# Attention and a gated feed-forward layer on one core: the output product in fifteen block products instead of seven

## The chip, the cores and the metric

The kernel runs on one core of a Trainium2 chip. The metric is the device time of one execution in microseconds (us), lower is better. TensorE (PE) does the matmuls into eight PSUM banks of 512 fp32 columns, VectorE (DVE) and ScalarE (ACT) the elementwise work, GpSimd (POOL) a part of it in the attention, and SyncE (SP) issues all transfers on one queue.

## What is computed

```python
scores = scale * q @ k.T + bias          # 8 x 8 heads, 576 tokens, head size 64
attn = softmax(where(mask, scores, -1e9))  # causal, window of 128
x = (attn @ v) -> [4608 tokens, 512]
gate = 1.0 / (1.0 + np.exp(-(x @ w_gate)))   # 512 x 1536
val = x @ w_val
out = (gate * val @ w_out)                   # 1536 x 512
```

All results are fp32. The weights come in fp64 and are decoded on the chip to fp32.

## The kernel before

The program is recorded as a graph of operations (`Graph.add`). `Graph.order` then chooses, with a cost written for each operation, which operation each engine issues next: the one that can start first, and among near equals the one with the smaller due time `want`. `SHIFTS` is a table of numbers that moves the due times of groups of operations. The instruction order on each engine is fixed by this when the program is built; on the chip each engine runs its own list and waits on semaphores.

There are three stages. In the **early stage** (to about 284 us) the attention of 32 pairs of heads runs beside the first third of the gate and value products (`gates1`, L631). In the **gate stage** (`gates2`, L716, to about 702 us) the rest of these products is made by seven block products for a 2x2 by 2x2 split, in token rounds of 2 x 512 or 2 x 384 (`HALVES`). The gated activations h (1536 x 4608, transposed) go out to DRAM in tiles `hs`. In the **output stage** (`results`, L842) out = w_out' h is made, again with seven products for a 2x2 by 2x2 split.

An fp32 operand is cut by `parts` into a high part (a cast, by `copy`, L263 on ACT or L264 on DVE) and a low part (a subtraction, `minus`, L273 on DVE, L272 on POOL). Each product of operands is three matmuls: high by high, low by high, high by low.

`results(t)` runs five times, for 2 x 512, 2 x 384, 2 x 384, 2 x 512 and 2 x 512 tokens. It loads the four quarters of h (two halves of the 1536 rows by two halves of the tokens) in thirds of 2 x 128 rows, 12 loads in each round, so 60 in all. The sums of quarters are made in place (L810), each operand is split into one of seven slots (`cxA`, `cxB`, `cxC`), and a product of 3 thirds and 2 row blocks of the output makes 36 matmuls. Evacuations scale or add from the bank into `ring` (L853 on ACT, L858 on DVE) and go to DRAM.

```python
for c in range(HC):
    for j, (xp, wp) in enumerate(((0, 0), (0, 1), (1, 0))):
        nc.tensor.matmul(mm[banks_[i]][:, a:b], wot(e * HC + c, wp)[:, k, i * P:(i + 1) * P], hcombo(s, xp)[:, c, a:b], ...)
```

The seven sums of the output weights are made by `combine`, in pieces of 256 elements, from `wod`, and stay in SBUF tiles `wos`, high and low, from the end of the gate stage on. The last evacuation of the program is cut in two halves of 256 columns (`halved`).

Of the kernel before, what the change touches and what calls it, by code (L numbers as in the profile page):

```python
# [15 lines left out]
P = 128  # L16
# [5 lines left out]
NT = B * S  # L22
# [9 lines left out]
HC = NFC // 6  # L32
NRING, NRING1, NHC = 6, 4, 7
# [208 lines left out]
def attention_gated_ffn(ctx: ExitStack, tc: tile.TileContext, qd, kd, vd, wg, wv, wo, out):  # L242
# [65 lines left out]

    xs = [dram.tile([KC, P, S], F32, name=f"xs{b}") for b in range(B)]
    hs = [[dram.tile([NFC // 2, P, HALVES[b // 2]], F32, name=f"hs{k}_{b}") for b in range(2 * NT2)] for k in range(2)]  # L310
    wod = [dram.tile([P, DM], F32, name=f"wod{f}") for f in range(NFC)]

# [757 lines left out]
```

## Time and profile before

| | |
|---|---|
| median of 3 runs | 968.12 us (967.6 to 968.31) |
| span of the profiled execution | 965.9 us, first to last instruction |
| PE busy | 959.7 us (99%) |
| DVE busy | 804.3 us (83%) |
| ACT busy | 512.5 us (53%) |
| granted TensorE clock | 0.999 of full speed |
| DMA | 162.70 MB, mean 168 GB/s |

The page gives the profiled execution by its span; the runs' times are those of whole executions and lie 1.7 to 2.4 us above that span. Busy times of matmuls are modelled and overlap, so the time between the starts of two matmuls tells more than the length of one. The chain of waits follows the end of the program back to what released each step.

### The profile page before, as it was taken

The page shows a single profiled execution, that of the slowest core. Times are in us where ns is not written, and L with a number is a line of the kernel's source. Part 1 is how long each engine was busy: PE and PEld are TensorE (multiplying, and loading weights), DVE is VectorE, ACT ScalarE, POOL GpSimd, SP SyncE. Part 2 cuts the span into 40 slices and gives each one's busy share as a digit, 9 for nine tenths or more (in the row PEclk, how much of TensorE's full clock was granted, in tenths as well). Part 3 has the DMA queues.
Part 4 walks back from the last instruction along what each step waited for, and adds up shares of the span by engine and source line. Part 5 has one row for each costly group of instructions (what it writes and reads, how often), then busy time and mean ns, then how long its engine had stood idle before and what let it go on. Part 6 is the DMA issues. An engine that isn't in the chain of part 4 may idle for free.

```text
span 965.9 us, 18563 instructions
## 1 busy us (share of the span) xinstructions
PE 959.7 (99%) x6576; PEld 819.3 (85%) x6576; DVE 804.3 (83%) x1950; ACT 512.5 (53%) x1319; POOL 168.6 (17%) x281
## 2 busy tenths in 40 slices
PE   9999999999999999999999999999999999999998
PEld 7777777787788889999988888888888999988887
DVE  7999989997879997795779648985999788799773
ACT  6998898987845563443435434532553223242231
POOL 7665454545311000000001000000200000000000
PEclk9999999999999999999999999999999999999999
DMA  8886769776436437763154413436245363737102
GB/s 303 277 268 234 262 237 312 247 241 209 147 112 189 161 96 244 241 228 123 42 161 126 147 55 119 138 104 207 98 147 165 119 180 98 222 106 239 37 8 88
DMA packets 83613, 162.70 MB, mean 168 GB/s; under 512 B 9408, under 2 KB 35008, under 8 KB 83520
## 3 DMA queue, kind: packets, MB, share of 16 engines
q1 hardware_dynamic: 83520, 161.51, 50.4%
q8 instruction: 52, 0.85, 0.4%
q14 instruction: 41, 0.34, 0.1%
HBM read 111.15 MB, written 50.33 MB: 167 GB/s over the span
## 4 chain that ended last, share of the span: by engine, by line
PE 92%; DVE 5%; ACT 2%; issue 1%; POOL 0%; ACTq 0%; POOLq 0%; DVEq 0%
PE mm L716 44%; PE mm L842 27%; PE mm L631 10%; PE mm L453 4%; PE mm L574 3%; PE mm L510 3%; DVE pb L468 1%; DVE mm L460 1%; ACT pb L471 1%; DVE work L373 1%; PE mm L551 1%; DVE x L273 0%; ACT pb L504 0%; DVE st L486 0%; ACT both L263 0%
## 5 line engine op out<-in xcount | busy, mean ns | idle before, releaser
L716 PE MATMUL mm<-cxA,w2s 128*128 128x512 f32 (+1 forms) x684 | 161.0, 372 | 0.0
L716 PE MATMUL mm<-cxB,w2s 128*128 128x512 f32 (+1 forms) x684 | 160.4, 372 | 0.0
L263 ACT COPY ring<-mm 128x512 f32<-128x512 f32 (+1 forms) x142 | 77.4, 551 | 129.4 <-PE mm L716 97.9
L716 PEld LDWEIGHTS mm<-cxA,w2s 128*128 128x128 f32 x684 | 125.8, 188 | 18.3
L716 PEld LDWEIGHTS mm<-cxB,w2s 128*128 128x128 f32 x684 | 125.8, 188 | 18.2
L631 PE MATMUL mm<-x,w 128*128 128x512 f32 x480 | 134.9, 411 | 0.3 <-DVE w L273 0.2
L521 POOL TENSOR_SCALAR_AFFINE_SELECT pt<-both 128x384 f32<-128x384 f32 x192 | 106.5, 579 | 82.9 <-ACT both L263 77.6
L471 ACT ACTIVATE pb<-pb,st 128x128 f32<-128x128 f32 x288 | 112.6, 395 | 10.1 <-DVE st L468 9.7
L842 PE MATMUL mm<-cxB,wos 128*128 128x512 f32 (+1 forms) x540 | 114.9, 367 | 0.0
L842 PE MATMUL mm<-cxA,wos 128*128 128x512 f32 (+1 forms) x540 | 114.4, 367 | 0.0
L842 PEld LDWEIGHTS mm<-cxB,wos 128*128 128x128 f32 x540 | 98.4, 188 | 12.7
L842 PEld LDWEIGHTS mm<-cxA,wos 128*128 128x128 f32 x540 | 98.4, 188 | 12.7
L631 PEld LDWEIGHTS mm<-x,w 128*128 128x128 f32 x480 | 83.8, 189 | 18.9 <-issue 3.9
L727 ACT ACTIVATE sg<-mm 128x512 f32<-128x512 f32 (+1 forms) x96 | 53.9, 563 | 65.9 <-PE mm L716 34.4
L272 POOL TENSOR_TENSOR work<-work 128x256 f32<-128x256 f32 x21 | 18.6, 889 | 376.2 <-DVE work L373 259.9
L723 DVE TENSOR_TENSOR mm<-mm,ring 128x512 f32<-128x512 f32 (+1 forms) x96 | 62.2, 648 | 26.0 <-PE mm L716 25.8
L373 DVE SCALAR_TENSOR_TENSOR work<-work 128x512 int32<-128x512 int32 x104 | 72.8, 711 | 0.8
L468 DVE CUSTOM_DVE_ANT_0 pb<-mm,relm 128x128 f32<-128x128 f32 x288 | 68.0, 279 | 0.0
L453 PE MATMUL mm<-kr,qr 64*64 64x192 f32 (+2 forms) x1280 | 63.1, 319 | 0.4 <-DVE st L488 0.2
L460 DVE COPY_PREDICATED mm<-swap,mm 128x256 f32<-128x256 int32 x144 | 54.5, 419 | 8.7 <-PE mm L453 8.5
L853 ACT ACTIVATE ring<-mm 128x512 f32<-128x512 f32 (+2 forms) x41 | 22.3, 547 | 65.3 <-PE mm L842 57.7
L453 PEld LDWEIGHTS mm<-kr,qr 64*64 64x64 f32 x1280 | 44.5, 134 | 13.3 <-issue 4.9
(117 smaller groups left out, 1576.6 us busy)
## 6 DMA issues: line engine op xcount, KB each, us to landing
hs<-ring SPq DMA_DIRECT2D x72, 256.0 KB, 2.0
kr<-in_k_dram SPq DMA_DIRECT2D x31, 576.0 KB, 5.5
work<-in_moe_w_gate_dram SPq DMA_DIRECT2D x20, 512.0 KB, 4.3
work<-in_moe_w_val_dram SPq DMA_DIRECT2D x20, 512.0 KB, 4.2
qr<-in_q_dram SPq DMA_DIRECT2D x31, 320.0 KB, 5.9
vr<-in_v_dram SPq DMA_DIRECT2D x32, 288.0 KB, 4.2
xs<-xt SPq DMA_DIRECT2D x32, 288.0 KB, 4.4
hr<-hs SPq DMA_DIRECT2D x18, 512.0 KB, 4.6
```

The lines of the kernel that those rows point to most:

```text
L263: g.add("ACT", act_cost(n, psum), lambda: nc.scalar.copy(out(), src()), reads, writes, want, release=release, guard=guard, ways=[("DVE", d ...
L373: g.add("DVE", dve_cost(DM, two=True), lambda word=word, scalar=scalar, o0=o0: nc.vector.scalar_tensor_tensor(bits(), wraw(s)[:, :, word], ...
L453: nc.tensor.matmul(sp[v.at][col, j, c0:c0 + n], qraw(u)[row, i // 2, col], kraw(u)[row, k1:k1 + n], start=True, stop=True)
L460: g.add("DVE", dve_cost(4 * D, psum=True), lambda b=b: nc.vector.copy_predicated(fold[b.at][:, :, 1:3], swaps, fold[b.at][:, :, 3::-3]), [ ...
L468: g.add("DVE", 0.21, lambda: nc.vector.tensor_tensor_reduce(pb()[:, e], sp[v.at][:, j, D:D + P], relm[u.p][:, w], op0=ALU.add, op1=ALU.min ...
L471: g.add("ACT", 0.39, lambda: nc.scalar.activation(pb()[:, e], pb()[:, e], AF.Exp, bias=st()[:, e:e + 1], scale=-1.0, accum_out=st()[:, 3 + ...
L521: nc.gpsimd.affine_select(pt(u)[:, f0:f0 + 2 * n - 1:2, :], both(), [[0, n], step], cmp, 0.0, base=0, channel_multiplier=mult)
L631: nc.tensor.matmul(psum(s)[:, 0:n], w1(kind, wi)[:, i, c * P:(c + 1) * P], x1(x)[:, c, 0:n], start=(k == 0 and c == 0), stop=(k == 2 and c ...
L716: nc.tensor.matmul(mm[b][:, 0:N], w2t(i, wp)[:, wk, c * P:(c + 1) * P], combo(k, xp)[:, c, 0:N], start=(start and c == 0 and j == 0), stop ...
L723: g.add("DVE", dve_cost(N, psum=True), lambda: nc.vector.tensor_tensor(o(), bk(b)(), a(), op=ALU.add), [("mm", b), *reads] if okeys else r ...
L727: g.add("ACT", act_cost(N, psum=True), lambda: nc.scalar.activation(sg[h](), bk(b)(), AF.Tanh, scale=0.5), [("mm", b)], [("sg", h)], F)
L842: nc.tensor.matmul(mm[banks_[i]][:, a:b], wot(e * HC + c, wp)[:, k, i * P:(i + 1) * P], hcombo(s, xp)[:, c, a:b], start=(start and e == c ...
```

## The change

The output product is cut otherwise: w_out' into 2 x 3 blocks (256 rows of the output by 512 of the 1536), h into 3 x 3 blocks (512 of the 1536 by 512 tokens). Three groups of 1536 tokens (`GRP3`) take the place of the five rounds. Fifteen products make a group, in the order `FLOW`; `FEED` names the operand of each, a block of h or one of the 13 sums `SUMS` (t0 to t12). A product is done in two halves e of the contraction (2 x 128 rows each), a half-product being 2 row blocks x 6 matmuls = 12 matmuls of 512 columns (L1012). So a group has 30 half-products.

Eleven sums of the weights (`WSUM`) are made once, in four pieces, during the gate stage (`wadd`, L823 and L824) and kept in DRAM (`wsum`). `wsplit` loads the 15 weight operands in the first group only, scales them by 0.5 or -0.5 into a high part (L845 on ACT, L846 on DVE) and a low part (L847 on DVE), which stay in SBUF (`wh`, `wl`, `w14`). `plan` hands out 14 buffers of 512 KB (`halfs`: 4 in `xr`, 4 in `work`, 6 in `hb`) for loads, sums (L1032) and weight operands; a block of h that is wanted again more than `KEEP` = 2 products later is loaded again. Four slots (`cxA` three, `cxC` one) take the split operands. `after` evacuates: banks are copied to `ring` or to another bank by ACT (`keep`, `seed`, L280), and DVE joins them (L926). The table `SHIFTS` is new as a whole. Where L273 and L263 stood, the low parts are L290 and the casts L280; L716 is now L742, L731 is L757.

```diff
-HC = NFC // 6
+GRP3 = 3 * NB
+FLOW = (8, 10, 9, 14, 7, 0, 2, 12, 1, 4, 5, 3, 11, 13, 6)
+FEED = ("t11", "h10", "h22", "t12", "t4", "t6", "t8", "h21", "t2", "t9", "t10", "t1", "t3", "h20", "h11")
+SUMS = {"t0": ("h12", 1, "h22"), "t1": ("h00", -1, "h20"), "t2": ("h02", -1, "h22"), "t3": ("h10", -1, "t0"), "t4": ("h01", 1, "t1"),
...
+KEEP, WLEAD = 2, 1
...
-    (3, 10), (5, 4), (9, -3), (10, 20), (11, -1), (12, -1), (13, -13), (14, -4), (15, -3), (17, 3), (18, 5), (21, -22), (22, 5), (24, 5), (25, -39),
...
+    (0, -21), (1, 114), (2, -60), (3, -47), (4, -10), (5, 388), (6, 37), (8, 76), (9, -18), (10, 115), (11, 74), (12, -25), (13, -56), (14, -11),
...
-    hs = [[dram.tile([NFC // 2, P, HALVES[b // 2]], F32, name=f"hs{k}_{b}") for b in range(2 * NT2)] for k in range(2)]
+    hs = [[dram.tile([KC, P, NB], F32, name=f"hs{k}_{b}") for b in range(NT // NB)] for k in range(NFC // KC)]
+    wsum = dram.tile([len(WMADE), KC, P, 2 * P], F32, name="wsum")
...
+    def wadd(c, wsrc):
...
+        move(lambda: as32(work()[:, 0:w0]).rearrange("p (j f) -> p j f", f=DM), lambda: wsrc[:, c].rearrange("j p f -> p j f"), ...
+        for o, a, sign, b in WSUM:
...
+            g.add("DVE", dve_cost(2 * P, two=True), lambda args=args: nc.vector.tensor_tensor(**args()),
+                  [(kw, a), (kw, b)], [(kw, o)], F, port=True, ways=[way])
+        move(lambda: wsum[:, c].rearrange("k p f -> p k f"), ...
...
+    def wsplit(n, at, wsrc):
...
+        g.add("ACT", act_cost(LN), lambda: nc.scalar.mul(wot(n, 0), val(), f), [("hq", at)], [("woh", n)], F,
+              ways=[("DVE", dve_cost(LN), True, lambda: nc.vector.tensor_scalar_mul(wot(n, 0), val(), f))])
+        g.add("DVE", dve_cost(LN, two=True), lambda: nc.vector.scalar_tensor_tensor(
+            wot(n, 1), val(), f, as32(wot(n, 0)), op0=ALU.mult, op1=ALU.subtract), [("hq", at), ("woh", n)], [("wol", n)], F, port=True)
...
+        home = {8: "A", 2: "A", 10: "B", 14: "B", 7: "B", 9: "C", 4: "C", 3: "C", 0: "D", 12: "D", 1: "E", 5: "E", 11: "F", 6: "F", 13: "G"}
+        fresh = (8, 10, 1, 11)
...
+        def after(t, k):
+            if k == 8:
+                seed("C", "A")
+            elif k == 10:
+                keep("s7", "B")
+            elif k == 14:
+                seed("D", "B")
...
+        def product(t, e, k, at):
+            q = seen[0] % len(pieces)
+            seen[0] += 1
+            parts(lambda: pieces[q](0), lambda: pieces[q](1), lambda: hv(at), m, [hk(at)], ("hc", q, 0), ("hc", q, 1), F)
...
+                        for d in range(2):
+                            for j, (xp, wp) in enumerate(((0, 0), (0, 1), (1, 0))):
+                                nc.tensor.matmul(mm[b][:, a:c], wot(n, wp)[:, 2 * e + d, i * P:(i + 1) * P], pieces[q](xp)[:, d, a:c],
+                                                 start=(k in fresh and e == d == j == 0), stop=(e == 1 and d == 1 and j == 2),
+                                                 skip_group_check=True)
```

How the order of instructions moves is shown at three places. On DVE in the output stage before, in a round of 2 x 384 tokens, sums (L810), low parts (L273) and casts (L264) of one operand follow each other, with an evacuation (L858) now and then:

```order
L273 TENSOR_TENSOR cxA<-hr,cxA 128x2x384
L810 TENSOR_TENSOR hr<-hr 128x2x384
L273 TENSOR_TENSOR cxA<-hw,cxA 128x2x384
L264 CAST cxC<-hr 128x2x384
L810 TENSOR_TENSOR hw<-hw,hr 128x2x384
L273 TENSOR_TENSOR cxC<-hr,cxC 128x2x384
L810 TENSOR_TENSOR hr<-hr 128x2x384
L264 CAST cxB<-hr 128x2x384
L273 TENSOR_TENSOR cxB<-hr,cxB 128x2x384
L858 SCALAR_TENSOR_TENSOR ring<-mm_141,ring 128x384
```

In the changed kernel the start of the first group, right behind the last gated product (L757), holds sums (L1032), low parts of activations (L290, into cxA and cxC) and parts of weights (L846, L847, into wh and wl):

```order
L757 SCALAR_TENSOR_TENSOR ring<-sg,ring 128x512
L290 TENSOR_TENSOR cxA<-hb,cxA 128x1024
L847 SCALAR_TENSOR_TENSOR wl<-xr,wh 128x1024
L1032 TENSOR_TENSOR hb<-hb,work 128x1024
L846 TENSOR_SCALAR wh<-hb 128x1024
L847 SCALAR_TENSOR_TENSOR wl<-hb,wh 128x1024
L290 TENSOR_TENSOR cxC<-hb,cxC 128x1024
L1032 TENSOR_TENSOR hb<-hb,xr 128x1024
L1032 TENSOR_TENSOR hb<-hb,work 128x1024
L290 TENSOR_TENSOR cxA<-work,cxA 128x1024
```

The parts of weights are in one queue with what the first products wait for; they stand in the first group alone.

On PE before, the end of product 0 and the start of product 4, which adds into the same bank mm_140 once ACT has copied that bank away (wos are the weight tiles, cxA and cxC the split activations):

```order
L842 MATMUL mm_140<-cxA,wos_7190 128x512 x3
L842 MATMUL mm_140<-cxA,wos_7242 128x512 x3
L842 MATMUL mm_141<-cxA,wos_7190 128x512 x3
L842 MATMUL mm_141<-cxA,wos_7242 128x512 x3
L842 MATMUL mm_140<-cxC,wos_6808 128x512 x3
L842 MATMUL mm_140<-cxC,wos_6990 128x512 x3
```

In the changed kernel the second half of product 10, in the banks mm_141 and mm_142, and behind it the start of product 14 in mm_141:

```order
L1012 MATMUL mm_141<-cxC,wl 128x512
L1012 MATMUL mm_141<-cxC,wh 128x512
L1012 MATMUL mm_142<-cxC,wh 128x512
L1012 MATMUL mm_142<-cxC,wl 128x512
L1012 MATMUL mm_142<-cxC,wh 128x512 x2
L1012 MATMUL mm_142<-cxC,wl 128x512
L1012 MATMUL mm_142<-cxC,wh 128x512
L1012 MATMUL mm_141<-cxA,wh 128x512
L1012 MATMUL mm_141<-cxA,wl 128x512
L1012 MATMUL mm_141<-cxA,wh 128x512 x2
```

In both, the six matmuls on the other bank are all that stands between the last matmul on a bank and the next that adds into it.

On ACT of the changed kernel, around the seeds of product 0 from the banks of product 14 (mm_141 to mm_143, mm_142 to mm_144):

```order
L280 CAST cxA<-xr 128x1024
L280 COPY ring<-mm_139 128x512
L280 COPY ring<-mm_140 128x512
L280 CAST cxA<-work 128x1024 x2
L280 COPY mm_143<-mm_141 128x512
L845 ACTIVATE wh<-hb 128x1024
L280 COPY mm_144<-mm_142 128x512
L845 ACTIVATE wh<-work 128x1024
L280 CAST cxC<-hb 128x1024
L845 ACTIVATE wh<-xr 128x1024
L280 CAST cxA<-hb 128x1024
```

The copies that PE waits for stand between casts (L280) and weight parts (L845); a copy from a bank to a bank had no counterpart in the old output stage.

## Rows read from the trace of the kernel before

**Rows 1.** the page's part on busy time and instructions of each engine

```profile
span 965.9 us, 18563 instructions
...
PE 959.7 (99%) x6576; PEld 819.3 (85%) x6576; DVE 804.3 (83%) x1950; ACT 512.5 (53%) x1319; POOL 168.6 (17%) x281
```

**Rows 2.** the chain that ended last, 690 to 966 us: start us, us, what

```profile
690.00 11.79 PE mm L716 x52
701.78 1.37 PE mm L842 x6
...
704.53 257.71 PE mm L842 x1260
...
962.26 0.38 ACT ring L853
```

**Rows 3.** the chain that ended last, 440 to 460 us, gate stage

```profile
439.91 20.11 PE mm L716 x116
```

**Rows 4.** groups by shape on PE, 440 to 460 us: shapes xcount | busy us, mean ns | idle

```profile
L716 PE MATMUL mm<-cxB,w2s 128*128 128x384 f32 x50 | 10.1, 334 | 0.0
```

**Rows 5.** groups by shape, output stage, 701 to 966 us

```profile
L842 PE MATMUL mm<-cxA,wos 128*128 128x512 f32 x324 | 76.0, 389 | 0.0
...
L842 PE MATMUL mm<-cxA,wos 128*128 128x384 f32 x216 | 38.8, 334 | 0.0
...
L842 PE MATMUL mm<-cxC,wos 128*128 128x512 f32 x102 | 24.9, 389 | 0.0
L273 DVE TENSOR_TENSOR cxB<-hr,cxB 128x1024 fp32r<-128x1024 f32 x18 | 21.9, 1219 | 1.2 <-ACT cxB L263 0.8
...
L853 ACT ACTIVATE ring<-mm 128x512 f32<-128x512 f32 x23 | 13.8, 599 | 46.8 <-PE mm L842 46.8
L263 ACT CAST cxB<-hr 128x1024 fp32r<-128x1024 f32 x13 | 13.5, 1051 | 38.1 <-PE mm L842 36.6 <-DVE hr L810 1.4
L842 PE MATMUL mm<-cxC,wos 128*128 128x384 f32 x72 | 13.4, 334 | 0.0
L858 DVE SCALAR_TENSOR_TENSOR ring<-mm,ring 128x512 f32<-128x512 f32 x18 | 12.4, 687 | 10.3 <-PE mm L842 10.3
...
L264 DVE CAST cxB<-hr 128x1024 fp32r<-128x1024 f32 x5 | 3.5, 691 | 0.8 <-PE mm L842 0.8
...
L842 PE MATMUL mm<-cxC,wos 128*128 128x256 f32 x12 | 1.6, 282 | 0.0
...
L727 ACT ACTIVATE sg<-mm 128x512 f32<-128x512 f32 x2 | 1.2, 600 | 1.4 <-DVE mm L723 0.8 <-PE mm L716 0.6
...
L731 DVE SCALAR_TENSOR_TENSOR ring<-sg,ring 128x512 f32<-128x512 f32 x1 | 0.7, 677 | 0.0
```

**Rows 6.** busy us of each engine by stretch, PEclk, DMA share, GB/s; last row: 701 to 966

```profile
0.00:100.00 100.00, 97.65 (x1096) 77.64 (x1096) 91.53 (x442) 86.66 (x333) 64.10 (x109) 1.00 0.79 270
...
600.00:700.00 100.00, 100.00 (x443) 82.81 (x442) 81.18 (x128) 44.08 (x67) 8.97 (x10) 1.00 0.44 147
...
sum 265.00, PE 261.22 PEld 231.24 DVE 214.84 ACT 85.81 POOL 0.00; mean PE 29.02 PEld 25.69 DVE 23.87 ACT 9.53 POOL 0.00
```

**Rows 7.** DVE's instructions in order of time: start us, us, what

```profile
851.38 1.22 DVE L810 TENSOR_TENSOR hr<-hr,hq 128x1024 f32<-128x1024 f32 x1
852.52 1.22 DVE L273 TENSOR_TENSOR cxA<-hw,cxA 128x1024 fp32r<-128x1024 f32 x1
...
861.60 1.21 DVE L273 TENSOR_TENSOR cxB<-hw,cxB 128x1024 fp32r<-128x1024 f32 x1
```

**Rows 8.** low parts on DVE by tile, 690 to 966 us, shapes merged

```profile
L273 DVE TENSOR_TENSOR cxB<-hr,cxB 128x1024 fp32r<-128x1024 f32 (+1 forms) x30 | 33.3, 1114 | 2.1 <-ACT cxB L263 1.2
...
L273 DVE TENSOR_TENSOR cxB<-hw,cxB 128x1024 fp32r<-128x1024 f32 (+1 forms) x15 | 16.6, 1112 | 0.7
```

**Rows 9.** transfers of the output stage: GB/s in 40 slices; issues, KB each, us to landing

```profile
GB/s 62 261 194 4 178 146 239 133 75 139 123 87 234 253 143 222 77 0 178 259 157 243 59 158 139 82 202 353 235 2 83 0 79 0 2 1 82 116 42 79
...
hr<-hs SPq DMA_DIRECT2D x12, 512.0 KB, 4.5
```

More of the change, by code (lines that the diff above doesn't have):

```diff
@@ L596, in attention_gated_ffn @@
     xrow = lambda: T(moe, "xr", [P, KC, 2 * N2], F32, tag="xr")
[L597 removed]
+    sgate = lambda s: T(moe, "sg", [P, 2 * NB], F32)[:, s * NB:(s + 1) * NB]
     def spill(src, key, fc, t0, n):
[L600 removed]
+        k, c = divmod(fc, KC)
         a = t0
         while a < t0 + n:
[L603 to L606 removed]
+            b = a // NB
+            e = min((b + 1) * NB, t0 + n)
+            move(lambda b=b, a=a, e=e: hs[k][b][c][:, a - b * NB:e - b * NB], lambda a=a, e=e: src()[:, a - t0:e - t0],
+                 [key], [("hs", k, b, c, a)], FIRST, (e - a) / 2)
+            spilt.setdefault((k, b, c), []).append(("hs", k, b, c, a))
             a = e
@@ new lines, in wadd @@
+    def wadd(c, wsrc):
+        F, kw = FIRST + 3.5, "wadd"
+        w0 = NFC // KC * DM
+        at = lambda x: as32(work()[:, x[1] * DM + x[0] * 2 * P:x[1] * DM + (x[0] + 1) * 2 * P] if isinstance(x, tuple) else
+                            work()[:, w0 + WMADE.index(x) * 2 * P:w0 + (WMADE.index(x) + 1) * 2 * P])
+        move(lambda: as32(work()[:, 0:w0]).rearrange("p (j f) -> p j f", f=DM), lambda: wsrc[:, c].rearrange("j p f -> p j f"),
+             [("wod", j * KC + c) for j in range(NFC // KC)], [(kw, (i, j)) for i in range(2) for j in range(NFC // KC)], F, 768)
+        for o, a, sign, b in WSUM:
+            op = ALU.add if sign > 0 else ALU.subtract
+            args = lambda o=o, a=a, b=b, op=op: dict(out=at(o), in0=at(a), in1=at(b), op=op)
+            way = ("POOL", 0.1 + 2 * P * 0.00223, True, lambda args=args: nc.gpsimd.tensor_tensor(**args()))
+            g.add("DVE", dve_cost(2 * P, two=True), lambda args=args: nc.vector.tensor_tensor(**args()),
+                  [(kw, a), (kw, b)], [(kw, o)], F, port=True, ways=[way])
+        move(lambda: wsum[:, c].rearrange("k p f -> p k f"), lambda: as32(work()[:, w0:w0 + len(WMADE) * 2 * P]).rearrange("p (k f) -> p k f", f=2 * P),
+             [(kw, o) for o in WMADE], [("wsum", c)], F, len(WMADE) * 128)
@@ new lines, in plan, with need @@
+    def plan():
+        steps = []
+        for t in range(NT // GRP3):
+            known = set()
+            for s, k in enumerate(FLOW):
+                todo = []
+                def need(v):
+                    if v in SUMS and v not in known:
+                        need(SUMS[v][0])
+                        need(SUMS[v][2])
+                        known.add(v)
+                        todo.append(v)
+                need(FEED[k])
+                for e in range(2):
+                    for v in todo:
+                        steps.append((t, s, e, v, (SUMS[v][0], SUMS[v][2])))
+                    steps.append((t, s, e, None, (FEED[k],)))
+        last = {}
+        for n, (t, s, e, v, ins) in enumerate(steps):
+            for x in ins:
+                last.setdefault((t, e, x), []).append((s, n))
+        idle = list(range(len(halfs)))
+        at, work_, fetched = {}, [], [0]
+        for n, (t, s, e, v, ins) in enumerate(steps):
+            mine, done = [], []
+            if t == 0 and s < len(FLOW) and s == fetched[0]:
+                for w in range(0 if s == 0 else s + WLEAD, s + WLEAD + 1):
+                    if w < len(FLOW):
+                        work_.append(("wload", t, e, w, idle[0]))
+                        idle.append(idle.pop(0))
+                fetched[0] += 1
+            for x in dict.fromkeys(ins):
+                key = (t, e, x)
+                if key not in at:
+                    at[key] = idle.pop(0)
+                    work_.append(("load", t, e, x, at[key]))
+                mine.append(at[key])
+                later = [z for z, m in last[key] if m > n]
+                if not later or x not in SUMS and later[0] - s > KEEP:
+                    done.append(at.pop(key))
+            if v:
+                o = done.pop(0) if done else idle.pop(0)
+                at[t, e, v] = o
+                work_.append(("add", t, e, v, (mine[0], mine[1], o)))
+            else:
+                work_.append(("use", t, e, FLOW[s], mine[0]))
+            idle += done
+        return work_
@@ L961, in attention_gated_ffn @@
     else:
-        wsrc = [wo[f] for f in range(NFC)]
+        wsrc = wo.rearrange("(j c) p f -> j c p f", c=KC)
+    spare = [("wraw", s) for s in range(NRAW)] + [("wbits", s) for s in range(2)] + [("tt", j) for j in range(2)]
+    wkeys = [("wadd", x) for x in (*WMADE, *((i, j) for i in range(2) for j in range(NFC // KC)))]
+    follow(spare, wkeys)
+    for c in range(KC):
+        wadd(c, wsrc)
+    follow(wkeys, spare)
     banks[0] = 8
```

279 lines of the change are left out of this document (157 added, 122 removed), and 56 rows, old and new, of the table SHIFTS.

## The prediction

> **What bounds the kernel now.** I read the parts of the span first, then the chain, then the shapes. TensorE (PE) is busy 99% of the span [rows 1], but a busy PE is not yet a full one, so the chain of waits decides. At the end of the program it is PE alone: 52 matmuls of the gate stage take 11.79 us, that is 226.7 ns from one start to the next, and from 701.78 us to 962.24 us the output stage (L842) follows with nothing between [rows 2]. In the gate stage 116 matmuls take 20.11 us, 173.4 ns each [rows 3], and the shapes of that stretch are all 128x384 [rows 4]. The two rates differ by 53.3 ns for 128 columns (0.4164 ns a column), so a matmul costs its columns plus 13.5 ns; one of 256 columns comes to an estimated 120 ns.
>
> Does that explain the whole output stage? Its shapes [rows 5] are 750 matmuls of 512 columns (cxB has the same rows as cxA), 504 of 384 and 12 of 256: 750 x 0.2267 + 504 x 0.1734 + 12 x 0.120 = 170.0 + 87.4 + 1.4 = 258.9 us. The chain has 1.37 + 257.71 = 259.1 us [rows 2]. So **PE never waits there**, and the stage is worth exactly its matmuls. VectorE (DVE) is second: 214.8 of 265 us [rows 6].
>
> **The change: matmuls.** Fifteen products of a 2x3 by 3x3 split replace seven of 2x2 by 2x2. In the order there are 1074 matmuls of 512 columns and 12 of 256 (the last evacuation is still cut in two): 1074 x 0.2267 + 1.4 = 244.9 us. Saved: 259.1 - 244.9 = **14.2 us**, if PE is still never kept waiting. Of this, 27,648 columns fewer give 11.5 us, and 180 matmuls fewer at 13.5 ns give 2.4 us; the rest is the 0.2 us by which the chain exceeds my model. That the change does not do what it says is excluded: the counts stand in the order.
> The Trainium skill (TensorE: Matmul & The Clock Gate, Back-to-back issue gap) gives a warm matmul N/2.4 + 2.5 ns. By that the stage would go from 245.1 to 233.1 us and save 12.0 us. The rows have 13.5 ns where the Trainium skill has 2.5, so I stay with the rows.
>
> **VectorE in the output stage.** Ten two-operand instructions on 1024 elements start from 851.38 to 861.60 us [rows 7], so 1.136 us apart, though each lasts 1.219 [rows 5]: neighbours overlap by 0.083 us. I take that off the other rows too: 0.604 us for 512 elements from PSUM, 0.608 for a cast. After the last instruction of the gate stage (L757) the new order has on DVE 88 low parts (L290), 75 sums (L1032), 8 weight parts (L847), 47 joins of 512, 2 of 256, 10 casts or scalings: 171 x 1.136 + 47 x 0.604 + 10 x 0.608 + 0.7 = 229.4 us, against 244.9 of PE. It fits in sum, but not evenly, since all weight parts stand in the first of the three token groups. A group has 30 half-products (15 products, two halves of the contraction) of 12 matmuls, 2.72 us each. Up to the low part of the 31st the order has 29 + 26 + 8 = 63 long instructions, one scaling and 14 joins: 71.6 + 0.6 + 8.5 = 80.7 us (the first two low parts are made earlier). PE needs 30 x 2.72 = 81.6 us to get there. DVE starts that count later than PE, since the last gate matmul is followed by tanh (0.60) and a product (0.68) [rows 5]: 80.7 + 1.3 = 82.0. **VectorE is at the edge for the first 80 us**: late by 0.4 us if it never waits. It does wait, for the cast of the high part on ScalarE (ACT): over the six groups of low parts in the old stage the idle time before them adds up to 8.5 us for 105, 0.08 us each [rows 8] (first and last shown); 30 of them make 2.4 us. Part of those waits came from VectorE being ahead, so I take half: 0.4 + 1.2 = **1.6 us of stall**, bounds 0 and 2.8. The other two groups have 56 long instructions and 16 joins, 73.3 us in 81.6, and cost nothing.
>
> **ScalarE's handovers.** Product 14 adds into the banks of product 10, and product 7 into those of product 14, once ACT has copied the bank away. In the new PE order only one group of 6 matmuls (1.36 us) stands between, for about three banks in each token group, nine in all. If ACT is free, a copy of 0.60 fits; if a cast has just begun, 1.05 + 0.60 - 1.36 = 0.29 us is lost [rows 5]. A copy from PSUM to PSUM is in no row; I price it as the copy to SBUF. Bounds 0 and 2.6 us. The old order has the same handover in its first round (product 0 to product 4, one group between), and the old chain shows no gap, so I take **0.3**.
>
> **What is covered.** The sums of the output weights (42 of 256 elements on DVE) and the first 7 low parts of weights move into the gate stage: 17,920 two-operand elements, where 25 old sums and 11 old low parts had 16,896. At 1.136 us for 1024 that is 1.1 us more, with three scalings about 3 us. DVE is busy 81.2 of 100 us there [rows 6], and what hides it is PE's own matmuls; without that cover the 3 us would be on the path. Four reads of the weights, four stores of their sums and some smaller stores join SP's queue in the same stage, behind whose waits the gate stage's stores and loads stand; its transfers keep the DMA engines 44% busy [rows 6], and I put it at nothing. The tail has one join of 256 elements and its store where 0.38 us of scaling and a store were [rows 2]: unchanged.
>
> **The early stage.** The table of shifts is new, so scores, softmax and first gates stand in another order: 73 row scalings on DVE instead of 97, 132 on ACT instead of 115. Its work is the same. PE is without work for 2.35 us in the first 100 [rows 6], so little can be won: bounds 2.5 us better, 3 us worse, and I take 0.
>
> **Sum.** 14.2 - 1.6 - 0.3 = 12.3 us less. The profiled execution has a span of 965.9 us, so 953.6; the median of the runs, 968.12, lies 2.2 us above that span, hence **955.8 us**.
>
> **Rivals.**
> *VectorE becomes the bound.* By the durations of the rows, overlap not taken off, its work is 171 x 1.219 + 47 x 0.687 + 10 x 0.691 + 0.9 = 248.5 us, more than PE's 244.9. With the 1.3 us of lag the stage takes 249.8, and 9.3 us are saved: 958.8; with waits at 0.08 us for all 90 low parts 966. For it: the first group is at the edge. Against: the timeline shows the overlap. I give it 0.17, at 959 to 966.
> The Trainium skill (Perfetto Trace Analysis, Identifying the Most-Contended Engine) takes the share of busy time as a fair measure of how near VectorE is to its limit. By that rule this rival is the forecast; the starts in [rows 7] speak against it.
> *The loads come late, and it is slower.* The stage now fetches 105 blocks of 512 KB (90 of the activations, since the sums reload them, and 15 of weights) where 60 stood, 24 of them smaller. The order issues 21 of them ahead of the last gate store; 84 remain, and one takes 4.5 us from issue to landing [rows 9]. One at a time that is 378 us. SP issues in order, and each load waits until VectorE has released one of 14 buffers. With fewer than 378 / 259.1 = 1.46 in flight on average the stage is longer than before; at 1.4 it takes 270 us, so 979 us. Against: a slice of 353 GB/s [rows 9] is three such loads at once (512 KB in 4.5 us is 116 GB/s). Chance 0.06.
> *The early order is worse.* Chains through DVE and ACT lengthen by 4 us or more: 960 to 967. Nothing in the rows points there, and nothing forbids it. Chance 0.09.
>
> **Chances and range.** The forecast (stalls of at most 5 us) has 0.68, at 952.5 to 959. No change is 0.2%, 1.9 us, about what a measurement tells apart; only the edges of the first and third rival reach it: 0.03. Slower by more: the loads and a remainder of the early order, 0.07. Faster by more: 0.90. The low end is no stall (953.9) with about half of the early gain, 952.5; the high end, 962.5, reaches into VectorE's and the early rival; left out are the loads (0.06) and the far parts of the other two.
>
> **What would show it.** Right: 1086 matmuls at L1012 on an unbroken chain of about 245 to 248 us, single gaps within the first 85 us of it, ended by VectorE's L290; the gate stage without gaps as before; VectorE near 100% busy in that first third and lower after. Wrong: gaps ended by DMA into hb, work or xr (the loads); gaps in the second and third group (VectorE's sum); PE's first output matmul well after or before 702 us (the early order); waits on ACT's copies of banks above 3 us (handovers).

## The result, and the profile after

The changed kernel takes **956.34 us** (median of 4 runs, 955.84 to 958.19) against 968.08 for the kernel before on the same chip: a ratio of 0.9882, 95% interval 0.9868 to 0.9896. Two later repeats gave 0.9891 (0.9878 to 0.9905) and 0.9888 (0.9873 to 0.9903). So it is faster by 10.6 to 11.7 us (968.43 - 957.63, 967.73 - 957.14 and 968.08 - 956.34 are 10.8, 10.6 and 11.7). The forecast was 955.8.

The page of the changed kernel, its part on busy time, answers to [rows 1]:

```profile
span 956.2 us, 18327 instructions
...
PE 946.9 (99%) x6396; PEld 790.7 (83%) x6396; DVE 823.4 (86%) x1938; ACT 546.0 (57%) x1367; POOL 177.0 (19%) x295
```

180 matmuls fewer, 9.7 us less of span. This profiled execution is the one of 958.19 us, the highest of the four, so it loses 1.4 to 2.4 us that the others don't.

To see where the time went, I summed the distances from the start of one matmul to the start of the next, by line, in the profiled execution of each kernel. This gives three stages: the gate stage (L716 before, L742 now), the output stage (L842, now L1012), and everything ahead of them.

```
us                        early   gate    output
before                    281.5   421.5   258.9
after                     278.6   427.0   246.7
forecast for after        281.5   421.5   246.8
```

The output stage came out as forecast. The early stage gained 2.9 us and the gate stage lost 5.5, both where the forecast had nothing. The last matmul starts 4.0 us before the span's end in both kernels, so the tail is unchanged, as forecast.

**The output stage.** The chain of waits of the changed kernel, 680 to 957 us (start us, us, what), answers to [rows 2]:

```profile
679.85 24.49 PE mm L742 x108
...
704.78 7.17 DMA hb<-wsum
...
711.98 0.71 DVE wh L846
...
713.85 0.89 DVE cxC L290
...
714.98 1.23 DVE hb L1032
...
717.19 0.58 ACT ring L280
...
717.82 234.72 PE mm L1012 x1038
```

Read it from the bottom. The last 1038 matmuls take 234.72 us, 226.1 ns each: no wait worth naming. Ahead of them the chain leaves PE for 13 us and goes back to a load of a weight sum that took 7.17 us to land. PE was working on the first two products meanwhile; what it lost, by the starts of its matmuls, is 0.96 us at 713.9, 0.29 at 717.3 and 0.15 at 718.2. The first of these waits ended with VectorE's low part, as the forecast had it (704 to 720 us: us in total, times, longest):

```profile
PE mm L1012 <- DVE cxC L290: 0.8, 1, 0.8
```

Busy time by stretch in the changed kernel (columns as in [rows 6]: PE, PEld, DVE, ACT, POOL, clock, DMA share, GB/s):

```profile
700.00:720.00 20.00, 19.09 (x82) 14.76 (x81) 18.43 (x21) 10.60 (x14) 0.00 (x0) 1.00 0.84 293
720.00:740.00 20.00, 20.00 (x90) 16.55 (x89) 20.00 (x19) 13.46 (x17) 0.00 (x0) 1.00 0.89 286
740.00:760.00 20.00, 20.00 (x90) 16.57 (x89) 20.00 (x21) 9.56 (x12) 0.00 (x0) 1.00 0.56 179
760.00:785.00 25.00, 25.00 (x112) 20.54 (x111) 25.00 (x28) 13.03 (x15) 0.00 (x0) 1.00 0.95 322
785.00:866.00 81.00, 81.00 (x359) 66.92 (x358) 79.38 (x80) 37.67 (x44) 0.00 (x0) 1.00 0.75 255
```

VectorE is busy for all of the 65 us from 720 to 785, and PE doesn't wait once there. A single engine at 100% next to another at 100% is possible when the two are just balanced. The Trainium skill (Perfetto Trace Analysis, Identifying the Most-Contended Engine) would have VectorE improved first, by its share; these rows do not bear out that it sets the pace there.

**The gate stage.** What the matmuls of the changed kernel waited for, 300 to 704 us: us in total, times, longest (PE, then the weight load ahead of it):

```profile
PE mm L742 <- ACT ring L280: 1.7, 3, 0.9
PE mm L742 <- DVE ring L749: 0.6, 1, 0.6
```
```profile
PEld mm L742 <- ACT ring L280: 3.2, 5, 1.2
PEld mm L742 <- DVE ring L749: 1.0, 1, 1.0
```

The forecast had this stage without gaps. Now PE waits for copies of its banks into the ring (L280, ACT), and some of these wait for a slot of the ring, which is held until its store into DRAM (hs) has landed. The chain of the changed kernel, 370 to 392 us, shows one such round:

```profile
374.72 4.36 DMA hs<-ring
...
379.16 0.49 ACT ring L280
...
379.69 10.74 PE mm L742 x60
```

Theory from these rows: the new transfers of the gate stage (the weights' sums, 3 MB read and 5.6 MB stored) delay those small stores; the early gain is the new table's; the stall at the start of the output stage is one late weight load and not VectorE's sum. Rivals: VectorE's added sums, or the table's order, make the gate stage's waits; VectorE is the bound at the start of the output stage. The ledger under experiment 3 shows that this theory holds for the smaller part of the gate stage's loss.

### The profile page after: what moved, and what is told of

Read it like the earlier page. It is cut to its first block, busy times and chain, and to the rows that moved or that the text cites. A ratio compares the mean times of both kernels' runs of the same rounds, so it can differ in the third digit from the quotient of the medians.

```text
span 956.2 us, 18327 instructions
## 1 busy us (share of the span) xinstructions
PE 946.9 (99%) x6396; PEld 790.7 (83%) x6396; DVE 823.4 (86%) x1938; ACT 546.0 (57%) x1367; POOL 177.0 (19%) x295
## 4 chain that ended last, share of the span: by engine, by line
PE 89%; DVE 5%; DMA 4%; issue 1%; ACT 1%; SPq 0%; POOL 0%; DVEq 0%; ACTq 0%; POOLq 0%
PE mm L742 38%; PE mm L1012 25%; PE mm L657 12%; PE mm L478 5%; PE mm L599 4%; PE mm L535 3%; DMA hs<-ring 2%; DMA xr<-xs 1%; PE mm L576 1%; DMA hb<-wsum 1%; PE mm L523 1%; DVE work L398 1%; DVE mm L485 1%; DVE pb L493 1%; PE mm L343 0%
## 5 line engine op out<-in xcount | busy, mean ns | idle before, releaser
L280 ACT COPY ring<-mm 128x512 f32<-128x512 f32 (+1 forms) x175 | 96.8, 560 | 163.6 <-PE mm L742 101.5
L1012 PE MATMUL mm<-cxA,wh 128*128 128x512 f32 x504 | 160.1, 390 | 0.1
L657 PE MATMUL mm<-x,wl 128*128 128x512 f32 x480 | 134.9, 411 | 0.0
L742 PE MATMUL mm<-cxB,wh 128*128 128x512 f32 (+1 forms) x504 | 117.6, 374 | 1.5 <-ACT ring L280 1.5
L742 PE MATMUL mm<-cxA,wh 128*128 128x512 f32 (+1 forms) x504 | 117.4, 374 | 0.0
L1012 PEld LDWEIGHTS mm<-cxA,wh 128*128 128x128 f32 x504 | 94.3, 188 | 20.9 <-DVE cxA L290 0.8
L1012 PE MATMUL mm<-cxA,wl 128*128 128x512 f32 (+1 forms) x274 | 106.2, 388 | 0.0
L742 PEld LDWEIGHTS mm<-cxB,wh 128*128 128x128 f32 x504 | 92.7, 188 | 16.3 <-ACT ring L280 2.1
L742 PEld LDWEIGHTS mm<-cxA,wh 128*128 128x128 f32 x504 | 92.8, 188 | 14.0
L657 PEld LDWEIGHTS mm<-x,wl 128*128 128x128 f32 x480 | 83.7, 188 | 19.0 <-issue 3.6
L742 PE MATMUL mm<-cxB,wl 128*128 128x512 f32 (+1 forms) x360 | 82.7, 369 | 0.3 <-ACT ring L280 0.3
L742 PE MATMUL mm<-cxA,wl 128*128 128x512 f32 (+1 forms) x360 | 82.4, 369 | 0.3 <-ACT sg L753 0.2
L742 PEld LDWEIGHTS mm<-cxB,wl 128*128 128x128 f32 x360 | 65.6, 188 | 10.0 <-ACT ring L280 1.1
L742 PEld LDWEIGHTS mm<-cxA,wl 128*128 128x128 f32 x360 | 65.7, 188 | 9.8 <-ACT sg L753 0.9
```

The source lines that it names most:

```text
L280: g.add("ACT", act_cost(n, psum), lambda: nc.scalar.copy(out(), src()), reads, writes, want, release=release, guard=guard, ways=[("DVE", d ...
L657: nc.tensor.matmul(psum(s)[:, 0:n], w1(kind, wi)[:, i, c * P:(c + 1) * P], x1(x)[:, c, 0:n], start=(k == 0 and c == 0), stop=(k == 2 and c ...
L742: nc.tensor.matmul(mm[b][:, 0:N], w2t(i, wp)[:, wk, c * P:(c + 1) * P], combo(k, xp)[:, c, 0:N], start=(start and c == 0 and j == 0), stop ...
L1012: nc.tensor.matmul(mm[b][:, a:c], wot(n, wp)[:, 2 * e + d, i * P:(i + 1) * P], pieces[q](xp)[:, d, a:c], start=(k in fresh and e == d == j ...
```

## The experiments

Times are medians; ratios are to the kernel before on the same chip. Stages are measured as above, each from one profiled execution.

**1. The changed kernel again** (no edit), twice.

> The changed kernel, nothing edited; a second profile of it. The ledger of the first profile by starts of matmuls is: before the gate stage 3.1 us less than in the kernel before, gate stage 5.5 us more (427.0 against 421.5), output stage 12.3 us less (246.7 against 259.0). Theory (the gaps belong to the order of the work): the same gaps stand at the same places, gate stage 425.5 to 428 us, output stage 246 to 247.5, median 955.5 to 957. Rival (the first profile caught a slow sample, its time was 1.8 us over the median): gate stage at most 424, the gaps at 378 and 390 us missing or at other places.

> The changed kernel once more, on the chip of the two kernels above, as their measure: gate stage 425 to 427 us, output stage 246.2 to 246.8, median 956 to 958.

Measured: 957.63 us (0.9891) with early 279.6, gate 425.5, output 246.3; and 957.14 us (0.9888) with 278.5, 425.6, 246.7. Gaps stood at 327.0, 379.4, 390.4, 410.0 and 432.1 us in the first, at 326.0, 378.2, 389.0, 409.0 and 463.6 in the second. Most gaps stand at the same work in all three profiles, so they belong to the kernel: the gate stage loses 3.9 to 5.5 us. The first repeat's median missed my range by 0.6 us (at most 957); the second repeat is inside all of its ranges. The first profile is the dearest of the three, as its time is.

In the chain of the first repeat, 400 to 440 us, the same round is seen twice, first with a copy on VectorE, then on ACT. The store at 401.45 stands behind a read of 512 KB of the output weights (issued at 400.00, landed at 404.00), which the kernel before has too. Only the store of 192 KB at 426.41 stands behind a store of the sums (issued at 421.28) and the next read (421.74):

```profile
401.45 4.41 DMA hs<-ring
...
426.41 5.87 DMA hs<-ring
...
432.30 0.49 ACT ring L280
...
432.83 7.21 PE mm L742 x39
```

**2. No sums.** The sums' operations stay in the plan and emit nothing:

```diff
+        for o in g.ops[mark:]: o.emit, o.ways = None, [(*way[:4], lambda: None) for way in o.ways]
...
```

> Left out: the sums of the output weights, their reads and their stores (42 sums on VectorE, a few on GpSimd, 4 loads, 4 stores); products with a summed weight read a block of the weights themselves, with pieces of the same length, so the output is not the reference's. The order of everything else is unchanged. Theory (the gate stage's gaps come from the sums and their transfers): gate stage at most 423 us, median 952 to 953.5. Rival 1 (the gaps come from ring slots held by the stores of the gated rows and from the new order): gaps at 326, 378 and 390 us stay, gate stage 425.5 us or more, median 955 to 956.5, so at most 1 us gained. Output stage 246 to 247.5 by both.

Measured: 955.62 us (0.9865, 0.9852 to 0.9879), gate stage 423.4 us, output stage 245.6. About 2 us of the gate stage's loss are gone, 1.9 are left. Neither theory had both parts: the stage is in reach of the first (at most 423), the median is in the range of the rival (955 to 956.5), and the gain of 2.0 us over the repeat lies between the two. The output stage, which both had at 246 or more, gained 0.7 to 1.1: a first hint that its stall hangs on the loads. The summed weights' two loads into hb, read here from another tensor in pieces of the same 1 KB, landed in 5.8 to 6.5 us.

**3. No stores of the sums.** The sums and their reads stay, the four stores don't.

```diff
+        for o in g.ops[-1:]: o.ways = [(*way[:4], lambda: None) for way in o.ways]
...
```

> Left out: only the four stores of the weight sums (1408 KB each); the sums themselves, on VectorE and GpSimd, and the reads for them stay. Products with a summed weight read a block of the weights instead, so the output is not the reference's. Theory (transfers: the stores of the gated rows into DRAM take 2.6 to 3.9 us beside the sums' transfers, against 1.7 to 1.9 without, and hold the ring's slots): gate stage 423 to 424.5 us, most of what leaving out the sums altogether gave (423.4); small stores between 410 and 475 us back near 2.5 us or less. Rival (VectorE's 42 sums are what keeps the gate stage): gate stage 425.5 us or more, as in the changed kernel, although the stores are short.

Measured: 955.47 us (0.9876, 0.986 to 0.9891), gate stage **422.8** us, just under the theory's range and far from the rival's. VectorE still does its 42 sums, and the stage is as short as without them, so VectorE's sums are not what costs. The issues between 410 and 475 us show what the stores of the sums do (KB each, median us from issue to landing), first in the first repeat of the changed kernel:

```profile
wsum<-work SPq DMA_DIRECT2D x4, 1408.0 KB, 6.1
...
hs<-ring SPq DMA_DIRECT2D x8, 192.0 KB, 2.6
hs<-ring SPq DMA_DIRECT2D x9, 128.0 KB, 3.7
...
hs<-ring SPq DMA_DIRECT2D x8, 64.0 KB, 3.9
```

and without the sums' stores:

```profile
hs<-ring SPq DMA_DIRECT2D x8, 192.0 KB, 1.9
hs<-ring SPq DMA_DIRECT2D x9, 128.0 KB, 1.7
...
hs<-ring SPq DMA_DIRECT2D x9, 64.0 KB, 1.6
```

A store of 64 KB takes 3.9 us where it takes 1.6 without them. How much of the gate stage's loss is this? I summed what each matmul of the stage took beyond 226.7 ns (512 columns) or 173.4 ns (384 columns), in three stretches. The sums run in the middle one: in the first repeat their first read is issued at 409.67 us, their first store at 421.28. Experiments 5 to 9 come below; 8 has the sums later.

```
us lost by the gate stage     to 411   411 to 520   behind
before                          0.1        0.2        0.0
changed kernel                  3.4        2.0        0.4
first repeat                    2.6        1.2        0.4
second repeat                   3.0        1.1        0.3
experiment 5                    3.3        1.8        0.2
experiment 6                    1.6        2.0        0.4
experiment 7                    2.1        2.2        0.3
experiment 9                    3.3        1.2        0.4
2, no sums                      1.3        0.7        0.1
3, no stores of the sums        1.1        0.4        0.2
8, sums later                   2.4        3.6        3.7
8, later and long pieces        2.4        2.5        4.1
```

In the middle stretch the six profiles with the sums' stores on SP's queue lose 1.1 to 2.2 us, the two without these stores 0.4 and 0.7: about 1 us is what the sums' transfers are shown to cost in this order. The larger part is lost ahead of 411 us, before any transfer of the sums but the first read, and it is there with the sums left out (1.3) or moved away (2.4) too. Its cause is open. The chains show small stores that land late behind reads and stores of the output weights' decoding, but the kernel before has these transfers in the same stretch, and ACT waited longer for such stores there without a gap on PE. Two things that differ were not tested apart: the order of the first 130 us of the stage, and the smaller pieces in which the gated rows go out (34 stores between 290 and 411 us where 28 stood). And the two profiles without the sums' stores are of the fastest execution of their kernel (954.06 and 953.72 us against medians of 955.62 and 955.47), so part of their shorter stage can be chance.

**4. Empty tables of shifts**, in the changed kernel and in the kernel before.

```diff
-SHIFTS = (
...
+SHIFTS = ()
```

> The changed kernel with an empty table of shifts. Read against the kernel before with an empty table. Theory (what the change adds to the gate stage causes the waits there, the new table wins 3 us in the early stage): with both tables empty the change is worth 12.3 - 5.5 = 6.8 us, between 5.5 and 8. Rival (the new table's order causes the gate waits as well as the early gain): with both tables empty the change is worth 11 to 13.5 us, and the gate stage takes the same time in both kernels within 1 us. The output stage should be 246 to 249 us, whatever the table.

> The kernel before with an empty table of shifts, the other half of the comparison. Both theories: slower than the kernel before, by 2 to 20 us, nearly all of it before the output stage; the output stage stays at 259 to 260 us.

Measured: 965.82 us (0.9979, 0.997 to 0.9988) for the changed kernel, 978.31 us (1.0103, 1.0087 to 1.0118) for the kernel before.

```
us, empty table           early   gate    output
before                    289.1   424.3   258.7
after                     289.7   426.0   246.7
```

Without tables the change is worth 978.31 - 965.82 = 12.5 us, in the rival's range and far from the 5.5 to 8 of the theory. The output stage alone is worth 258.7 - 246.7 = 12.0. By the medians the two other stages together thus gain about 0.5 us without tables; with them they lose 0.5 to 1.9 (12.2 to 12.6 in the output stage, 10.6 to 11.7 in all). So the change is worth 0.8 to 1.9 us less with the tuned orders than without, and a part of the loss in these stages comes with them.

Which stage that share lies in, these two profiles don't settle. Their stages differ by 9.7 us in all, not 12.5, since the profiled execution of the changed kernel took 968.12 us, 2.3 over its median. These 2.3 us lie in one of its stages, and the early stage differs by up to 3 us between executions of the same early order. So the equal early stages (+0.6) don't show that the gain of 1.9 to 3.0 us in the early stage is the new table's alone, and the 1.7 us between the gate stages, more than the 1 us the rival allowed, may be less. What the profiles do show: the kernel before, without its table, has gate waits of its own, 1.05 us at 424.8 and 1.19 at 435.4 (gate stage 424.3 instead of 421.5). So waits in this stage come with the order and not only with the new work.

**5. The sums' store in long pieces.**

```diff
-    wsum = dram.tile([len(WMADE), KC, P, 2 * P], F32, name="wsum")
+    wsum = dram.tile([KC, P, len(WMADE), 2 * P], F32, name="wsum")
...
```

> The sums lie in DRAM so that a row of all eleven sums is contiguous: the four stores of 1408 KB are written in pieces of 11 KB instead of 1 KB, the loads still read pieces of 1 KB. Nothing else changes. Theory (transfers in the gate stage): the sums' store lands in 5 us or less instead of 6.1, the small stores beside it wait less, gate stage 424 to 425 us, 0.5 to 1.5 us faster than the changed kernel. Rival (VectorE, or the number of bytes and not of pieces): gate stage 425.5 to 427, the store's landing within 0.5 us of 6.1, same time.

Measured: 957.76 us (0.9888, 0.9873 to 0.9903), gate stage 426.4 us; the store landed in 5.8 us instead of 6.1, the small stores in 3.0 to 3.4. The rival holds: pieces eleven times as long gain nothing here that can be told from the repeats. Whether the bytes set the landing was not tested.

**6. The loads of summed weights in long pieces.**

```diff
+    wsum = dram.tile([len(WMADE), P, KC, 2 * P], F32, name="wsum")
...
+            move(val, lambda: wsum[WMADE.index(k)], [("wsum", c) for c in range(KC)], [("hq", at)], F, 512)
...
```

> The sums lie in DRAM so that the block of one product is contiguous for each partition: the eleven loads of summed weights read pieces of 4 KB instead of 1 KB, the stores still write pieces of 1 KB. Nothing else changes. Theory (the stall at the start of the output stage, 1.4 to 1.8 us, comes from the third product's weights, which land 6.8 to 7.2 us after issue): they land in 5.5 us or less, output stage 245.2 to 245.9 us instead of 246.3 to 246.7. Rival (VectorE is at its limit there): the load may land sooner, the output stage stays at 246.2 to 247.

Measured: 955.58 us (0.9872, 0.9857 to 0.9886), output stage **245.6** us. The landing of the two loads into hb fell from 6.7 us (the changed kernel, 700 to 960 us) to 5.4 (this one, 695 to 960):

```profile
hb<-wsum SPq DMA_DIRECT2D x2, 512.0 KB, 6.7
```
```profile
hb<-wsum SPq DMA_DIRECT2D x2, 512.0 KB, 5.4
```

VectorE's instructions in order of time show what this does. In the first repeat of the changed kernel VectorE idles 0.28 and 0.34 us for loads just ahead of the low part cxC, for which PE waits:

```profile
709.49 1.23 DVE L1032 TENSOR_TENSOR hb<-hb,work 128x1024 f32<-128x1024 f32 x1 [0.28 <-DMA hb<-hs]
711.06 0.69 DVE L846 TENSOR_SCALAR wh<-hb 128x1024 fp32r<-128x1024 f32 x1 [0.34 <-DMA hb<-wsum]
711.79 1.23 DVE L847 SCALAR_TENSOR_TENSOR wl<-hb,wh 128x1024 fp32r<-128x1024 f32 x1
712.93 1.22 DVE L290 TENSOR_TENSOR cxC<-hb,cxC 128x1024 fp32r<-128x1024 f32 x1
```

With long pieces there is no such wait:

```profile
710.66 1.22 DVE L1032 TENSOR_TENSOR hb<-hb,work 128x1024 f32<-128x1024 f32 x1
711.80 0.69 DVE L846 TENSOR_SCALAR wh<-hb 128x1024 fp32r<-128x1024 f32 x1
```

The gap of PE at 713.4 us in the repeat is gone. What is left, 0.28 us at 717.2 and 0.14 at 718.1, stands in every kernel with the fifteen products: a copy of a bank on ACT behind a cast of 1.06 us, which itself began late because VectorE's sum came late.

**7. Less work for VectorE.** The low parts of the last eight weight blocks are left out.

```diff
-        g.add("DVE", dve_cost(LN, two=True), lambda: nc.vector.scalar_tensor_tensor(
+        g.add("DVE", dve_cost(LN, two=True), lambda: None if n > 6 else nc.vector.scalar_tensor_tensor(
```

> Left out: the low parts of the last eight weight blocks (8 instructions of 1.14 us on VectorE in the first third of the output stage), so the output is not the reference's. Order otherwise unchanged. Theory (after the first 20 us of the output stage VectorE keeps up, no gap is left to win; the stall comes from a late load): output stage 245.8 to 246.9 us, no gain of more than 0.6 us in the stage. Rival of the prediction (VectorE is the bound in the first third): 9 us less of its work leave no gap, output stage at most 245.4 us.

Measured: 956.19 us (0.9876, 0.9862 to 0.9889), output stage 245.4 us: by my bounds the rival's result. But the rival said that VectorE is short of time through the first third, and nine microseconds less of its work gave one microsecond. The gain is all at one place, 713 us, where the wide loads gave it too. The first of the eight low parts stood ahead of the last gate instructions; without it VectorE reached the weights of the third product 1.5 us earlier (709.60 us, not 711.06), and the buffer it reads was free sooner (the load of the next weight sum was issued at 701.48 us, not 702.30). The kernel took away work and advanced a load at once, so it doesn't separate the two theories; experiment 6 does, since it left VectorE's work alone.

**8. The sums later**, behind the first round of new gate weights (each operation keeps its number for the table of shifts); and this together with the long pieces.

```diff
                 instead(held + 3, new + 3)
+                if t == EARLY:
+                    sums()
...
```

> The sums of the output weights, with their reads and stores, are planned behind the first round of new gate weights instead of ahead of it: in the trace of the changed kernel that is the stretch from 541 to 604 us, where the DMA engines are 11 to 24% busy and VectorE 38 to 82%, instead of 410 to 475 us (48 to 87%). The table of shifts stays on the same instructions. Theory (the sums' transfers hold up the stores of the gated rows while these are short, and the ring with them): small stores between 410 and 475 us back to 2.5 us or less, no gaps of over 0.3 us behind 410 us, gate stage 422.8 to 424.5 us, output stage 246.2 to 246.8, 1.5 to 3 us faster than the changed kernel. Rival (the waits move along with the sums): gaps between 541 and 610 us, gate stage 425.5 us or more, same time.

> Both together: the sums later, and the block of one product contiguous for each partition, so that the loads of summed weights read pieces of 4 KB. Theory: the two gains add up, gate stage 422.8 to 424.5 us and output stage 245.4 to 245.9 us, 2 to 4 us faster than the changed kernel. Rival (the output stage's stall stays, since the load is behind the gate stage's last stores on SP's queue all the same): output stage 246.2 us or more.

Measured: 962.41 us (0.9941, 0.9928 to 0.9953), gate stage 430.8 us, output stage 246.4; and 960.69 us (0.9929, 0.9916 to 0.9941), 430.1 and 245.6. Worse by 5.3 and 3.6 us than the changed kernel on the same chip, so this idea for a faster version failed. Waits came in the new place, as the rival said, and more came in the old one: 1.78 us at 471.6, 1.68 at 564.6. In the new place the stores of the gated rows are of 256 KB and land in 4.8 us (541 to 610 us; 2.0 from 300 to 700 us in the kernel without sums):

```profile
hs<-ring SPq DMA_DIRECT2D x14, 256.0 KB, 4.8
```

But the wait at 564.6 has no store in its chain (545 to 570 us); it goes from PE through two of VectorE's instructions back to PE:

```profile
544.85 20.19 PE mm L742 x89
...
565.06 0.71 DVE mm L749
...
565.79 0.70 DVE ring L757
...
566.53 3.47 PE mm L742 x14
```

In the old place the theory's sign was there: between 410 and 475 us the stores of 64 and 128 KB landed in 1.8 us, those of 192 KB in 3.6. PE lost more all the same. The wait at 471.6 us hangs on one slow store (chain, 440 to 480 us):

```profile
468.85 4.17 DMA hs<-ring
...
473.10 0.49 ACT ring L280
...
473.64 6.52 PE mm L742 x34
```

No large transfer was near it: the last read of gate weights in that stretch had landed at 425.4 us. Beside the other small stores the trace has only one transfer of instructions then, of 16 KB and 1.8 us, which began at 469.9 (463 to 475 us):

```profile
q8 instruction: 1, 0.02, 0.9%
```

Both kernels have 16 such transfers between 290 and 705 us, of 0.9 to 1.8 us each, and another fell into the late store at 374.72 us of the changed kernel (376.8 us). Whether they hold up the stores was not tested.

A stretch in which DMA and VectorE look idle in the mean isn't one in which PE has slack. In the output stage the pair shows experiment 6 again: 246.4 with short pieces, 245.6 with long ones.

**9. The sums' stores from GpSimd's queue**, with the long pieces of experiment 6.

```diff
+        o = g.ops[-1]; o.ways = [(*w, lambda: [nc.gpsimd.dma_start(wsum[a:e, :, c].rearrange("k p f -> p k f"), as32(work()[:, w0 + a * 2 * P:w0 + e * 2 * P]).rearrange("p (k f) -> p k f", f=2 * P)) for a, e in ((0, 6), (6, 11))]) for *w, _ in o.ways]
...
```

> The contiguous blocks for the loads of summed weights, and besides the four stores of the sums are issued by GpSimd in two pieces each (768 and 640 KB) instead of by SP; the place of everything else in the order is unchanged. SP waits 16 us in all for the sums in front of these stores, and the stores of the gated rows stand behind them on its queue. Theory A (the queue is what counts: the stores of the gated rows wait behind the sums' stores on the same queue): small stores between 410 and 475 us land in 2.5 us or less after issue, no gap over 0.3 us between 410 and 510 us, gate stage 423 to 424.5 us, output stage 245.4 to 245.9; 2 to 3.5 us faster than the changed kernel. Theory B (the DMA engines' time is what counts, whatever the queue): small stores still 2.6 to 4 us, gate stage 425 us or more; then only the output stage's 0.7 us are gained. A cost that neither has: GpSimd's own part of a store could hold up VectorE; it would show as VectorE instructions longer than their usual 0.68 and 0.42 us beside it.

Measured: 957.45 us (0.9886, 0.9869 to 0.9902), gate stage 426.0, output stage 245.6. Between 410 and 475 us:

```profile
hs<-ring SPq DMA_DIRECT2D x8, 192.0 KB, 2.6
hs<-ring SPq DMA_DIRECT2D x9, 128.0 KB, 3.0
...
hs<-ring SPq DMA_DIRECT2D x9, 64.0 KB, 2.8
```

For 64 KB that is between the 3.9 on one queue and the 1.6 without: the queue, or the smaller pieces, has a part in it, the rest stays with two queues. VectorE's sums took 423 ns beside GpSimd's issues, no longer than in the first repeat (435). The gate stage is no shorter, as theory B had it; its largest gap, 0.97 us at 409.7, lies ahead of the first of these stores, where most of the loss is.

No version here beats the changed kernel by more than the intervals: the best that computes the same, experiment 6, has 0.9872 (0.9857 to 0.9886) against 0.9882, 0.9891 and 0.9888. Its output stage is shorter by 0.7 to 1.1 us in each of three kernels; its ratio is lower by 0.0010 to 0.0019 (1.0 to 1.8 us), which fits that but lies within the intervals.

## Why the prediction was right, point by point

- **Matmuls of the output stage, -14.2 us: right.** 245.6 us with long pieces, of which 0.4 to 0.5 is gaps, against 244.9 by the sum. With the Trainium skill's gap (TensorE: Matmul & The Clock Gate, Back-to-back issue gap) the stage would be 233.1 us; this trace does not agree, the 13.5 ns a matmul from the rows hold. The section gives that formula for an isolated gap, and for a stream of weight loads and matmuls about 131 ns at 512 columns; here each matmul has its weight load, and they start 226 to 227 ns apart. That the formula's saving of 12.0 us lies near the measured 12.2 to 12.6 is an accident: these include the stall.
- **VectorE's stall, +1.6 us, and ScalarE's handovers, +0.3: near in size (1.4 to 1.8 over 244.9 for both, where 1.9 was forecast), the stall wrong in place and partly in cause.** The step that failed is "late by 0.4 us if it never waits", plus waits for casts spread over 80 us. VectorE kept up through these 80 us, and all stalls came within 14 us of the start; 0.7 to 1.1 us were one load of weights, which SP issued only 0.8 us ahead of the first output matmul, next behind a load for which it had waited until a matmul of the gate stage was done.
- **ScalarE's handovers by themselves:** 0.28 and 0.14 us at one place, nearly by the mechanism named (the cast ahead of the copy had waited for VectorE's sum), not at all nine.
- **Covered work, 0: the term that failed.** The gate stage lost 3.9 to 5.5 us. I costed the sums' instructions on VectorE and their place on SP's queue, and put the transfers "at nothing" because the DMA engines are 44% busy. About 1 us of the loss is these transfers (experiment 3): a mean share says nothing about a store of 64 KB behind one of 1408 KB, and I did not ask what that store holds: a slot of the ring, for which ACT waits, for which PE waits. The rest, 2.6 to 3.4 us ahead of 411 us, is lost before the sums' transfers, and the forecast has no term for it at all: "the gate stage without gaps as before" took the old order's slack for granted in a new order. Its cause is open. The sign that slack was used there was in the trace of before (ACT, 300 to 700 us: us in total, times, longest), where PE had no gap:

```profile
ACT ring L263 <- DMA hs<-ring: 28.0, 17, 4.4
```

- **Early stage, 0: a gain of 1.9 to 3.0 us,** beyond the lower bound of 2.5 in two of three profiles. Whether it comes from the new table alone is not shown (experiment 4), and which chains got shorter was not traced.
- The two misses, about -2.6 and +4.5 us, mostly cancel; with the output stage at -12.4 (means of the three profiles) that makes -10.5, beside the measured 10.6 to 11.7. That the result lies so close to 955.8 is in good part luck.
- **The signs.** The chain of the output stage, the place of its gaps and VectorE's 100% came as the signs of being right had them. Two signs of being wrong came too: a load into hb at the root of the first gap, and the first output matmul at 704.1 to 705.5 us, which was late through the gate stage and not, as the sign said, through the early order.
- **The rivals.** VectorE as the bound: no, 65 us at 100% without a gap on PE. Loads late through the whole stage: no; one load, at its start. Early order worse: the opposite.

## What to carry to other kernels

When work is moved under a busy engine, cost its transfers by what they delay: list the small transfers that share their queue, the buffer that each of them holds, and who waits for that buffer. A mean DMA share of 44% and an idle stretch of VectorE were no evidence of slack, in the forecast and in the attempt to repair it alike. Before a loss is put down to new work, look where it lies: most of it lay ahead of that work here. And compare two tuned orders with the tuning taken out of both, with more than one profile each: one profile that is 2 us over its median can't tell the order's gains from the edit's costs.

## What the runs showed of the hardware that was not expected

- Stores of 64 KB landed 3.9 us after issue (median of 8) in a stretch with stores of 1408 KB on the same queue, and in 1.6 without these; with the large stores on another queue and in halves it took 2.8.
- Long pieces helped these loads and hardly these stores: 512 KB read in pieces of 4 KB landed in 5.4 us instead of 6.7 to 6.9 with 1 KB (5.1 instead of 6.9 in the kernels of experiment 8), while 1408 KB written in pieces of 11 KB took 5.8 instead of 6.1. The length of a piece isn't all of it: the same loads from another tensor, in pieces of 1 KB, landed in 5.8 to 6.5 (experiments 2 and 3).
- Profiled executions with the same early order differ by up to 3 us in the early stage alone (278.5 to 281.5 us over eleven profiles), so differences of 1 us are read better from a stage than from the median, and for a stage that varies so, from several profiles.
